# A new order of work and loads for the first two blocks of an attention, MoE and expert-mixture kernel

## The chip, the cores and the metric

The kernel runs on one core of one Trainium2 chip. The metric is the device time of one execution in microseconds, the median of three runs. A core has TensorE (PE, its weight loads shown as PEld), VectorE (DVE), ScalarE (ACT), GpSimd (POOL) and SyncE (SP, which here only issues transfers). Each engine carries out its own list of instructions strictly in the order in which the program wrote it, and waits on semaphores for what the others give it.

## The reference

All data are drawn at random; the attention part is linear, without a softmax.

```python
kv  = einsum('bhsd,bhse->bhde', k, v)          # q, k, v: (4, 8, 576, 64)
out = einsum('bhsd,bhde->bhse', q, kv)
out = out / sqrt(mean(out**2, -1) + 1e-6) * g_norm
x   = out as (2304, 512)
h   = max(x @ w1, x @ w2, x @ w3)              # (2304, 768), float64 weights
y   = h @ w_out                                # (2304, 512)
p   = probs / (probs.sum(-1) + 1e-9)
out = sum over 4 experts e of p[:, e] * (relu(y @ e_w1[e]) @ e_w2[e])
```

## The kernel before

The 2304 rows are worked on in six blocks of 384. The first stage does the attention of all rows, and beside it the first MoE for blocks 0 and 1; blocks 2 to 5 of the first MoE follow, then the expert mixture in 24 rounds. Only the first stage is touched by the change. It is a list of steps, one word each, in the string `steps`; a loop goes through it and writes the instructions of each step, so the string sets the order on every engine.

The steps of the attention, with the lines that issue them: **K**bc multiplies k and v of batch b for a pair of heads, c from 0 to 3, into PSUM bank 7 (L269, 20 products of 64x64 in the profile); after c = 3 four copies bring the bank into the tile `kvb` (L68, one 64x256 copy each). **T**g transposes tile g of q in two halves (L295, 8 products), each half copied out to `qT` (L68 on ACT, L70 on DVE). **O**g multiplies `qT` and `kvb` into two banks (L319, 16 products; L311 for the half tiles 2 and 7), squares the result on ACT (L332) and sums the squares on DVE (L333, L334). **N**g takes the root on ACT (L342) and scales the banks on DVE (L343 to L346, then L353 twice). **X**g transposes the scaled tile (L362, 8 products, 4 for a half tile) and copies it out with the gain `g2` as a factor (L366 on ACT, L368 on DVE) to `yT`. Letters behind a dot name the engines of a step's copies: a for ACT, v for DVE, p for POOL, and so K13.vvaa has its first two kvb copies on DVE.

`g2` is loaded from `g_norm` by two small transfers that follow the first call of `pump()`, and is doubled on DVE:

```python
pump()
for h in range(2):
    nc.sync.dma_start(out=g2[h * D : (h + 1) * D, :], in_=g_norm.rearrange("(d o) -> d o", o=1))   # L660
nc.vector.tensor_scalar(out=g2, in0=g2, scalar1=2.0, scalar2=None, op0=ALU.mult)                    # L661
```

The first MoE in this stage: **S**j splits block j of x into a high and a low part (L70, L376), **A**ijf makes the product of block j with slice f of weight i (L247, 12 products of 128x384; i = 0 is copied out, 1 and 2 are combined by a maximum on DVE, L392), **H**jf splits the maximum (L70, L401), and **P**f multiplies it with w_out (L413, 12 products). The weights come as float64, 24 pieces of 512 KB (L176 to the tiles `stage`). Each is converted by a scaling on ACT (L197) and a minimum on POOL (L198), then three integer operations on DVE (L205, L206, L209), then split into a high part (L68 or L70) and a low one (L183). In the kernel before, step a takes one piece through its split and the next through its first part, and step b does the DVE work.

All loads go through SP in the order of the string `order` (k, q or w for a weight piece): a load waits for its buffer, and eight transfers can be under way before SP waits for the oldest of them. `pump()`, called after each step, issues all loads whose buffers are free. After the loop PE goes on with block 2 (the row at 165.74 us below).

Of the kernel before, what the change touches and what calls it, by code (L numbers as in the profile page):

```python
# [8 lines left out]
F32 = mybir.dt.float32  # L9
# [12 lines left out]
def tile_attn_moe_moe2(  # L22
# [23 lines left out]
    nc = tc.nc  # L46
    B, H, S, D = q.shape
    NT, DM = out.shape
    FF = w1.shape[1]
    E, _, EF = e_w1.shape  # L50
    P = 128
# [3 lines left out]
    T = 384  # L55
# [3 lines left out]
    NPAIR = H // 2  # L59
    KC = S // P  # L60
    EPS = 1e-6

    def f32(ap):
        return ap.bitcast(F32)

    def copy(eng, out, in_):
        if eng == "a":
            nc.scalar.activation(out=out, in_=in_, func=AF.Copy)  # L68
        else:
            (nc.vector if eng == "v" else nc.gpsimd).tensor_copy(out=out, in_=in_)  # L70
# [7 lines left out]
    banks = [ps.tile([P, 512], F32, name=f"bank{n}") for n in range(8)]  # L78
# [7 lines left out]
    ident = cst.tile([P, P], F32, name="ident")  # L86
# [14 lines left out]
    def part(t, at, n, c=None):  # L101
        ap = t[:, at : at + n]
        return ap if c is None else ap.rearrange("p (c f) -> p c f", c=c)
# [13 lines left out]
    for b0 in range(0, B, 2):  # L117
        for b, s0 in ((b0, 0), (b0, 256), (b0, None), (b0 + 1, 0), (b0 + 1, 256)):
# [3 lines left out]
            else:  # L122
                rows = out[b * S + s0 : b * S + s0 + 256, :].rearrange("(p r) d -> r p d", r=2)
# [3 lines left out]
    kv_sb = {}  # L127
# [18 lines left out]
    HALF = P // 2  # L146
    KS = P * KC

    def load_kv(pool, b, c):
        for src, nm in ((k, "k"), (v, "v")):  # L150
            t = pool.tile([P, 4, KC + 1, D], F32, tag="kv", name=f"{nm}{b}_{c}", bufs=6)
            rows = src[b, 4 * c : 4 * c + 4]
            nc.sync.dma_start(out=t[:, :, 0:KC, :], in_=rows[:, 0:KS, :].rearrange("h (p c) d -> p h c d", c=KC))
            nc.sync.dma_start(out=t[0:HALF, :, KC, :], in_=rows[:, KS:S, :].rearrange("h p d -> p h d"))  # L154
            kv_sb[nm, b, c] = t
# [3 lines left out]
    worder = [("a", 0, 0)]  # L159
    for f in range(NF):  # L160
        worder += [("a", 1, f), ("a", 2, f)] + [("a", 0, f + 1)] * (f + 1 < NF) + [("o", 0, f)]
    N1 = 4 * NF
# [16 lines left out]
    def split_h(w, t, eng="a"):  # L179
        copy(eng, w[:, 0, :], t)  # L180

    def split_l(eng, w, t, key):
        eng.tensor_tensor(out=w[:, 1, :], in0=t, in1=f32(w[:, 0, :]), op=ALU.subtract)  # L183
        wt[key] = w

    def new_w(key):
        return w_buf[worder.index(key)]
# [4 lines left out]
    conv = {}  # L192

    def conv0(pool, key):
        words = stage[key].bitcast(I32).rearrange("p (n t) -> p n t", t=2)
        t = pool.tile([P, DM], F32, tag="cv", name="cv_" + "_".join(map(str, key)))
        nc.scalar.activation(out=t, in_=words[:, :, 1].bitcast(F32), func=AF.Abs, scale=2.0**-112)  # L197
        nc.gpsimd.tensor_scalar(out=t, in0=t, scalar1=EXP_TOP, scalar2=None, op0=ALU.min)  # L198
        conv[key] = t

    def conv1(pool, key):
        cpos[2] += 1
        words = stage.pop(key).bitcast(I32).rearrange("p (n t) -> p n t", t=2)
        ti = conv[key].bitcast(I32)
        nc.vector.tensor_scalar(out=ti, in0=ti, scalar1=3, scalar2=None, op0=ALU.logical_shift_left)  # L205
        nc.vector.scalar_tensor_tensor(  # L206
            out=ti, in0=words[:, :, 0], scalar=29, in1=ti, op0=ALU.logical_shift_right, op1=ALU.bitwise_or
        )
        nc.vector.scalar_tensor_tensor(  # L209
            out=ti, in0=words[:, :, 1], scalar=-(2**31), in1=ti, op0=ALU.bitwise_and, op1=ALU.bitwise_or  # L210
        )

    cpos = [0, 0, 0, 0]

    def conv_a(pool, eng="ap"):

        rest = []
        if cpos[3] < cpos[2]:  # L220
            key = worder[cpos[3]]
            w, t = new_w(key), conv.pop(key)
            split_h(w, t, eng[0])
            cpos[3] += 1
            if eng[1] == "p":
                split_l(nc.gpsimd, w, t, key)
            else:
                rest.append(lambda: split_l(nc.vector, w, t, key))
        if cpos[2] < cpos[1]:
            key1 = worder[cpos[2]]  # L230
            rest.insert(0, lambda: conv1(pool, key1))
        if cpos[1] < cpos[0]:
            conv0(pool, worder[cpos[1]])
            cpos[1] += 1
        return rest

    def load_w_to(pool, n):
        while cpos[0] < min(n, N1):
# [60 lines left out]
    def att_O(pool, kvb, gi):  # L299
# [30 lines left out]
        for i in range(nbank):  # L330
            sq = xt[:, i]
            nc.scalar.activation(out=sq, in_=o[i], func=AF.Square)  # L332
            nc.vector.reduce_sum(out=ss[:, i, :], in_=sq, axis=AX.X)  # L333
        nc.vector.tensor_scalar(out=a, in0=ss, scalar1=1.0 / D, scalar2=EPS, op0=ALU.mult, op1=ALU.add)  # L334
        xtok[gi] = (xt, ss, a, o, dst, small)
# [45 lines left out]
    nm = [0]  # L381

    def moe1_a(i, j, f, xs, eng="a"):

        ps = bank("a")
        col_mm(ps[:, :T], wt["a", i, f], xs)
        if i == 0:
            ms[j, f] = part(fa, NB * KT + nm[0] % 2 * T, T)
            nm[0] += 1
            copy(eng, ms[j, f], ps[:, :T])  # L390
        else:
            nc.vector.tensor_tensor(out=ms[j, f], in0=ps[:, :T], in1=ms[j, f], op=ALU.max)  # L392
# [225 lines left out]
    with tc.manual_schedule():  # L618
        cv_cm = tc.tile_pool(name="cvp", bufs=3, reuse_waits="tile")
        cvp = cv_cm.__enter__()  # L620
# [2 lines left out]
        att_cm = tc.tile_pool(name="att", bufs=2, side="right")  # L623
        att = att_cm.__enter__()
        make_identity(nc, ident)
        nc.gpsimd.memset(eps, EPS)

        nc.scalar.activation(out=g2, in_=ident[:, 0:1], func=AF.Sqrt)
        kvb = [att.tile([P, H * P + P], F32, name=f"kvb{i}", bufs=1) for i in range(2)]
        for t in kvb:  # L630
# [1 line left out]


        order = (
            "k00 q0 k01 q1 q2 k10 k11 q3 q4 q6 k20 q5 k21 k30 k31 w w w q8 q9 w"
        ).split()
        free = {"q": 6, "k": 3}

# [28 lines left out]
        def new_acc(n):  # L667
            return [bank("acc") for c in range(n)]
# [7 lines left out]


        steps = (
# [8 lines left out]
        ).split()  # L687
        for st in steps:
            st, *en = st.split(".")
            kind, at = st[0], [int(x) for x in st[1:]]  # L690
            if kind == "T":
                att_T(xq, *at, *en)
                free["q"] += 1
            elif kind == "K":
                att_kv(kvb, *at, *en)
                free["k"] += at[1] % 2
            elif kind == "O":
                att_O(xq, kvb, *at)
                if at[0] == len(groups) - 1:
                    att_cm.__exit__(None, None, None)  # L700
                    wp = ctx.enter_context(tc.tile_pool(name="wp", bufs=1, side="right", reuse_waits="tile"))
                    wr.append(wp.tile([P, 16 * 2 * DM], F32R, name="wr"))
                    w_buf.extend(part(wr[0], n * 2 * DM, 2 * DM, 2) for n in range(16))
            elif kind == "X":
                att_X(*at, *en)
                if at[0] == len(groups) - 1:
                    xq_cm.__exit__(None, None, None)
                    hs_cm = tc.tile_pool(name="hs", bufs=NF, side="right", reuse_waits="tile")
                    hs = hs_cm.__enter__()
            elif kind == "N":  # L710
                att_N(*at)
            elif kind == "A":
                i, j, f = at
                moe1_a(i, j, f, xs[j], *en)
            elif kind == "H":
                j, f = at
                hidden[j, f] = moe1_split(hs if j else None, j, f, *en)
            elif kind == "P":
                acc = acc or new_acc(KD)
                moe1_o(*at, hidden.pop((0, *at)), acc)  # L720
            elif kind == "S":
                xs.append(split_x(*at, *en))
            elif kind == "a":
                rest = conv_a(cvp, *en)
            elif kind == "b":
                for fn in rest:
                    fn()
            pump()
        assert cpos[3] == N1
        cv_cm.__exit__(None, None, None)  # L730
        moe1_store(0, acc)
        xs = xs[2]
        h = moe1_h(None, 2, 0, xs)
# [12 lines left out]
        for j in range(2, NB):  # L746
            acc = new_acc(KD)
            for f in range(NF):
                if j > 2 or f:
                    h = moe1_h(None, j, f, xs)  # L750
# [36 lines left out]
        for e in range(E):  # L787
            for pr in range(NPR):
                n = (e * NSB - 1) * NPR + pr
# [11 lines left out]
        for n, (e, sb, pr) in enumerate(rounds):  # L801
            last_sb = sb == NSB - 1
            more = not (e == E - 1 and last_sb)
            rest = iter(())
            if before is not None:
                e0, sb0, pr0 = before
                rest = second(n - 1, pr0)
# [60 lines left out]
```

## Time and profile before

| | |
|---|---|
| median of 3 runs | 1148.13 us (1147.34 to 1148.51) |
| the profiled execution: its own time | 1146.83 us |
| the profiled execution: span | 1145.0 us |
| PE busy in the span | 1120.5 us (98%), 6096 products |
| DVE / ACT / POOL busy | 562.7 / 390.9 / 236.8 us |
| the first stage, up to the first product of block 2 | 165.74 us |

The span runs from the first to the last instruction; the profiled execution's own time is 1.8 us longer. A busy share over the whole span says little about the first stage, which has other limits than the rest, so the rows below cut the span at the places where its limits change.

### The profile page before, as it was taken

What the parts mean: (1) busy time and instruction counts of PE and PEld (TensorE: products, weight loads), DVE (VectorE), ACT (ScalarE), POOL (GpSimd) and SP (SyncE); (2) the same over time, 40 slices, a digit from 0 to 9 for tenths busy, and PEclk for the clock granted to TensorE, in tenths of its full rate; (3) what the DMA queues carried; (4) which work ended last, traced back from release to release, by engine and by line L of the source; (5) the groups of instructions that cost most, each with busy time, mean ns of one, the idle gap of its engine ahead of it and who ended that gap; (6) DMA issues with size and microseconds to landing.
All of it is one profiled execution on the core that took longest, in us unless ns stands there. A gap on an engine that the chain in (4) does not pass through costs nothing.

```text
span 1145.0 us, 15032 instructions
## 1 busy us (share of the span) xinstructions
PE 1120.5 (98%) x6096; PEld 1031.7 (90%) x6096; DVE 562.7 (49%) x842; ACT 390.9 (34%) x699; POOL 236.8 (21%) x178
## 2 busy tenths in 40 slices
PE   6999899999999999999999999999999999999998
PEld 5888899999999888889888988888888888888887
DVE  1889862222325544344754436573535576343523
ACT  3653321121113434253634233452424253332321
POOL 1356740000401320205220202412020522011000
PEclk9999999999999999999999999999999999999999
DMA  9934410000201402014140403332030625040111
GB/s 255 283 107 130 147 47 29 1 28 1 65 29 37 157 1 102 9 56 138 60 171 1 165 1 131 127 122 99 29 138 9 212 65 193 1 153 14 48 63 56
DMA packets 77990, 99.59 MB, mean 87 GB/s; under 512 B 10336, under 2 KB 53344, under 8 KB 77920
## 3 DMA queue, kind: packets, MB, share of 16 engines
q1 hardware_dynamic: 77920, 98.62, 27.0%
q8 instruction: 48, 0.79, 0.3%
q14 instruction: 22, 0.18, 0.0%
HBM read 75.01 MB, written 23.59 MB: 86 GB/s over the span
## 4 chain that ended last, share of the span: by engine, by line
PE 88%; DVE 5%; DMA 2%; SPq 2%; ACT 1%; issue 1%; POOL 1%; DVEq 0%; ACTq 0%
PE bank L575 35%; PE bank L535 30%; PE bank L247 15%; PE bank L413 6%; DMA v<-in_v_dram 1%; DVE cv_a L206 1%; DVE cv_a L209 1%; PE bank L269 1%; DMA k<-in_k_dram 1%; PE bank L362 1%; DVE cv_a L205 1%; SPq L154 0%; PE bank L319 0%; DVE fa L392 0%; SPq L135 0%
## 5 line engine op out<-in xcount | busy, mean ns | idle before, releaser
L575 PE MATMUL bank<-wr,hr 128*128 128x512 f32 x792 | 227.0, 395 | 0.0
L559 DVE TENSOR_TENSOR fa<-bank,fa 128x384 f32<-128x384 f32 x144 | 80.1, 557 | 212.5 <-ACT fa L556 119.2
L575 PEld LDWEIGHTS bank<-wr,hr 128*128 128x128 f32 x792 | 147.0, 188 | 20.7
L517 POOL TENSOR_TENSOR fa<-fa 128x768 f32<-128x768 f32 x48 | 97.3, 2037 | 300.2 <-DMA fa<-y_d 243.0
L247 PE MATMUL bank<-xr,wr 128*128 128x384 f32 x792 | 145.2, 340 | 5.6 <-DVE fa L392 2.2
L247 PEld LDWEIGHTS bank<-xr,wr 128*128 128x128 f32 x792 | 139.6, 188 | 8.4 <-DVE fa L392 3.2
L486 POOL TENSOR_TENSOR w1s<-w1s 128x256 f32<-128x256 f32 x64 | 53.9, 862 | 421.8 <-DMA w1s<-in_moe_w_dram 374.7
L556 ACT ACTIVATE fa<-bank 128x384 f32<-128x384 f32 x144 | 70.6, 490 | 194.3 <-PE bank L535 194.3
L535 PE MATMUL bank<-rb,wr 128*128 128x384 f32 x648 | 131.5, 338 | 0.3 <-DVE hr L543 0.3
L535 PE MATMUL bank<-xr,wr 128*128 128x384 f32 x648 | 131.6, 338 | 0.0
L535 PEld LDWEIGHTS bank<-rb,wr 128*128 128x128 f32 x648 | 116.6, 188 | 10.2 <-DVE hr L543 0.6
L535 PEld LDWEIGHTS bank<-xr,wr 128*128 128x128 f32 x648 | 116.7, 188 | 9.6
L575 PE MATMUL bank<-wr,xr 128*128 128x512 f32 x324 | 100.8, 396 | 0.0
L392 DVE TENSOR_TENSOR fa<-bank,fa 128x384 f32<-128x384 f32 x72 | 39.8, 555 | 117.7 <-PE bank L247 117.5
L247 PE MATMUL bank<-xr,wl 128*128 128x384 f32 x504 | 90.5, 335 | 0.0
L247 PEld LDWEIGHTS bank<-xr,wl 128*128 128x128 f32 x504 | 87.4, 188 | 0.2 <-DVE wl L183 0.2
L575 PE MATMUL bank<-wl,hr 128*128 128x512 f32 x288 | 86.3, 394 | 0.0
L543 DVE SCALAR_TENSOR_TENSOR hr<-fa,hr 128x384 fp32r<-128x384 f32 x72 | 50.0, 695 | 42.6 <-ACT hr L542 42.6
L575 PEld LDWEIGHTS bank<-wr,xr 128*128 128x128 f32 x324 | 60.7, 188 | 10.8
L542 ACT ACTIVATE hr<-fa 128x384 fp32r<-128x384 f32 x72 | 37.8, 525 | 77.4 <-DVE fa L559 77.4
L575 PEld LDWEIGHTS bank<-wl,hr 128*128 128x128 f32 x288 | 53.4, 188 | 6.9
L542 ACT ACTIVATE xr<-fa 128x384 fp32r<-128x384 f32 x48 | 25.2, 525 | 96.7 <-DVE fa L559 96.7
(132 smaller groups left out, 1477.5 us busy)
## 6 DMA issues: line engine op xcount, KB each, us to landing
fa<-y_d SPq DMA_DIRECT2D x22, 768.0 KB, 6.2
stage_a<-in_moe_w_dram SPq DMA_DIRECT2D x18, 512.0 KB, 3.4
o_d<-fa SPq DMA_DIRECT2D x36, 256.0 KB, 3.7
fa<-o_d SPq DMA_DIRECT2D x36, 256.0 KB, 5.3
w1s<-in_moe_w_dram SPq DMA_DIRECT2D x32, 256.0 KB, 3.1
w2s<-in_moe_w_dram SPq DMA_DIRECT2D x32, 256.0 KB, 4.0
y_d<-fa SPq DMA_DIRECT2D x6, 768.0 KB, 3.8
o_d<-ob SPq DMA_DIRECT2D x18, 256.0 KB, 2.0
```

What stands on the lines that cost most here:

```text
L205: nc.vector.tensor_scalar(out=ti, in0=ti, scalar1=3, scalar2=None, op0=ALU.logical_shift_left)
L247: nc.tensor.matmul(ps, w[:, wi, c * P : (c + 1) * P], x[xi][:, c, :], start=(n == 0), stop=(n == 3 * KD - 1),)
L392: nc.vector.tensor_tensor(out=ms[j, f], in0=ps[:, :T], in1=ms[j, f], op=ALU.max)
L413: nc.tensor.matmul(acc[c][:, :T], w[:, wi, c * P : (c + 1) * P], h[hi], start=(f == 0 and n == 0), stop=(f == NF - 1 and n == 2),)
L486: eng.tensor_tensor(out=st[:, o], in0=st[:, a], in1=st[:, b], op=ALU.subtract)
L517: eng.tensor_tensor(out=yb[:, o], in0=yb[:, a], in1=yb[:, b], op=op)
L535: nc.tensor.matmul(out, w[wi][:, c * P : (c + 1) * P], y[yi][:, c, :], start=(i == 0 and k in BEGIN), stop=(i == 5), skip_group_check=k no ...
L542: nc.scalar.activation(out=h[0], in_=src, func=AF.Relu)
L543: nc.vector.scalar_tensor_tensor(out=h[1], in0=src, scalar=0.0, in1=f32(h[0]), op0=ALU.max, op1=ALU.subtract)
L556: nc.scalar.activation(out=s[k // 2], in_=a, func=AF.Copy)
L559: nc.vector.tensor_tensor(out=t, in0=x, in1=t, op=ALU.add)
L575: nc.tensor.matmul(banks[i], h[a, i // TPB][hi][:, i % TPB * P : (i % TPB + 1) * P], w[a][wi], start=(pr == 0 and a == 0 and m == 0), stop ...
```

## The change

Three things are new. Sixteen products of the identity matrix with itself are put ahead of everything on PE. The first k and v are loaded in parts by a function of their own, two of the parts issued by ACT's queue instead of SP's. And the two strings are written anew: the steps a and b are replaced by c (ACT and POOL part of a conversion), d (DVE part) and s (split), each with the number of its weight piece, and the engines of many copies are others.

```diff
+    WARM = 16
+    def load_first(pool):
+        ends = []
+        for src, nm, eng in ((k, "k", nc.sync), (v, "v", nc.scalar)):
+            t = pool.tile([P, 4, KC + 1, D], F32, tag="kv", name=f"{nm}0_0", bufs=6)
+            rows = src[0, 0:4]
+            parts = [
+                (t[:, 2 * i : 2 * i + 2, 0:KC, :], rows[2 * i : 2 * i + 2, 0:KS, :].rearrange("h (p c) d -> p h c d", c=KC))
+                for i in range(2)
+            ]
+            eng.dma_start(out=parts[0][0], in_=parts[0][1])
+            eng.dma_start(out=t[0:HALF, :, KC, :], in_=rows[:, KS:S, :].rearrange("h p d -> p h d"))
+            ends.append(parts[1])
+            kv_sb[nm, 0, 0] = t
+        for o, i in ends:
+            nc.sync.dma_start(out=o, in_=i)
     def load_kv(pool, b, c):
+        if (b, c) == (0, 0):
+            return load_first(pool)
...
-    def conv_a(pool, eng="ap"):
...
+    def conv2(key, eng="ap"):
+        w, t = new_w(key), conv.pop(key)
+        split_h(w, t, eng[0])
+        split_l(nc.gpsimd if eng[1] == "p" else nc.vector, w, t, key)
...
         make_identity(nc, ident)
+        for _ in range(WARM):
+            nc.tensor.matmul(banks[3][:, 0:P], ident, ident, start=True, stop=True)
...
-            "k00 q0 k01 q1 q2 k10 k11 q3 q4 q6 k20 q5 k21 k30 k31 w w w q8 q9 w"
+            "q1 q0 k00 k01 w q2 k10 k11 q3 w q4 k20 k21 q6 q5 k30 k31 w w q8 q9"
...
-            "K00 T0 K01 K02 K03 T1 O0 O1 K10 a N0 T2.av b K11 a N1 K12 K13 T3.av O2 b X0 N2 O3 T4 X1 "
+            "K00 K01 T1.av T0 K02 K03.avav c0 O1 O0 N1 K10 N0 T2 K11 d0 X1 K12 K13.vvaa T3.av X0.vv O3 T4.va "
...
-        assert cpos[3] == N1
+        assert cpos[2] == N1
```

On DVE, the first rows of its list; the names carry the program's numbers (bank7 is the bank of K, qT1 the transposed tile 1), and what a row waits for stands in brackets. Before:

```order
L661 TENSOR_SCALAR g2_75<-g2_75 128x1 [waits DMAHW3_49,DMAHW2_49,Activation_49]
L333 TENSOR_REDUCE ss0_253<-xt0_244 128x8 [waits Activation_49] x2
L334 TENSOR_SCALAR a0_254<-ss0_253 128x16 [waits DVE_49]
L333 TENSOR_REDUCE ss1_269<-xt1_260 128x8 [waits Activation_49] x2
L334 TENSOR_SCALAR a1_270<-ss1_269 128x16 [waits DVE_49]
```

On DVE, the same place after the change, where L667 is the former L661, L71 the former L70 and L337 the former L333:

```order
L667 TENSOR_SCALAR g2_75<-g2_75 128x1 [waits DMAHW6_49,DMAHW5_49,Activation_49]
L71 COPY qT1_210<-bank5_71 128x512 [waits PE_49]
L71 COPY kvb0_140<-bank7_73 64x4x64 [waits Activation_49] x2
L337 TENSOR_REDUCE ss1_274<-xt1_265 128x8 [waits Activation_49] x2
L338 TENSOR_SCALAR a1_275<-ss1_274 128x16 [waits DVE_49]
```

One copy of qT1 and two of kvb0 now stand on DVE behind the doubling of g2; before, ACT did all of these.

On SP, the end of the loads of batch 0 and what follows (v0_1 is v of the second half of the heads of batch 0; the short tail of a head has a load of its own). Before:

```order
L153 DMA v0_1_139<-in_v_dram 128x4x256
L154 DMA v0_1_139<-in_v_dram 64x4x64
L139 DMA q1_142<-in_q_dram 128x8x128
L135 DMA q2_144<-in_q_dram 32x8x128 x4
L153 DMA k1_0_149<-in_k_dram 128x4x256
L154 DMA k1_0_149<-in_k_dram 64x4x64
L153 DMA v1_0_152<-in_v_dram 128x4x256
L154 DMA v1_0_152<-in_v_dram 64x4x64
L660 DMA g2_75<-in_g_norm_dram 64x1 x2
```

On SP, after the change, where stage_a_0_0 is the first weight piece:

```order
L173 DMA v0_1_159<-in_v_dram 128x4x256
L174 DMA v0_1_159<-in_v_dram 64x4x64
L196 DMA stage_a_0_0_162<-in_moe_w1_dram 128x4x128
L136 DMA q2_164<-in_q_dram 32x8x128 x4
L173 DMA k1_0_169<-in_k_dram 128x4x256
L174 DMA k1_0_169<-in_k_dram 64x4x64
L173 DMA v1_0_172<-in_v_dram 128x4x256
L174 DMA v1_0_172<-in_v_dram 64x4x64
L666 DMA g2_75<-in_g_norm_dram 64x1 x2
```

The two loads of g2 keep their place behind k1_0 and v1_0; one weight piece has come in ahead of them, and q1 has gone to the front of the list.

On PE, the first rows before (ident is the identity matrix):

```order
L269 MATMUL bank7_73<-v0_0_131,k0_0_128 64x64 x10
L295 MATMUL bank4_70<-ident_74,q0_134 128x128 x4
L295 MATMUL bank5_71<-ident_74,q0_134 128x128 x4
L269 MATMUL bank7_73<-v0_0_131,k0_0_128 64x64 x10
L269 MATMUL bank7_73<-v0_1_139,k0_1_136 64x64 x20
L295 MATMUL bank6_72<-ident_74,q1_142 128x128 x4
L295 MATMUL bank4_70<-ident_74,q1_142 128x128 x4
L319 MATMUL bank0_66<-kvb0_124,qT0_168 128x128 x4
```

On PE, the same place after the change (a product of fp32 operands in K and O counts once here and twice in the profile):

```order
L631 MATMUL bank3_69<-ident_74 128x128 x16
L273 MATMUL bank7_73<-v0_0_151,k0_0_148 64x64 x20
L299 MATMUL bank4_70<-ident_74,q1_144 128x128 x4
L299 MATMUL bank5_71<-ident_74,q1_144 128x128 x4
L299 MATMUL bank6_72<-ident_74,q0_146 128x128 x4
L299 MATMUL bank4_70<-ident_74,q0_146 128x128 x4
L273 MATMUL bank7_73<-v0_1_159,k0_1_156 64x64 x20
L323 MATMUL bank0_66<-kvb0_140,qT1_210 128x128 x4
```

The sixteen identity products come first, both halves of k0_0 are multiplied at once, and O1 (L323) with kvb0 and qT1 is now ahead of O0.

## Rows read from the trace of the kernel before

**Rows 1.** Busy time by stage: stretch, its length, each engine, clock, DMA share, GB/s.

```profile
core 0: us, PE busy (x) PEld busy (x) DVE busy (x) ACT busy (x) POOL busy (x), PEclk, DMA share, GB/s
0.00:7.56 7.56, 0.00 (x0) 0.03 (x1) 0.00 (x0) 1.49 (x2) 2.71 (x9) 1.00 0.73 195
7.56:23.00 15.44, 14.53 (x129) 13.06 (x129) 0.00 (x0) 5.58 (x11) 1.04 (x1) 1.00 1.16 273
23.00:27.50 4.50, 3.04 (x56) 2.57 (x57) 3.55 (x11) 1.73 (x4) 0.00 (x0) 1.00 1.18 284
27.50:59.03 31.53, 28.26 (x356) 25.28 (x353) 25.38 (x53) 21.02 (x43) 11.35 (x5) 0.95 1.13 280
59.03:165.74 106.71, 101.24 (x596) 96.93 (x597) 95.47 (x151) 41.83 (x76) 70.68 (x51) 1.00 0.32 105
165.74:1145.00 979.26, 973.39 (x4969) 893.80 (x4968) 438.29 (x629) 319.25 (x564) 151.02 (x112) 1.00 0.22 74
```

**Rows 2.** Waits of PE in the first 200 us: total, times, longest.

```profile
PE bank L269 <- DMA v<-in_v_dram: 11.3, 4, 7.6
PE bank L247 <- DVE fa L392: 2.2, 3, 1.5
```

**Rows 3.** Timeline of PE: start, length, line, operation.

```profile
9.59 1.94 PE L295 MATMUL bank<-ident,q 128*128 128x128 f32 x8 [0.49 <-DMA q<-in_q_dram]
18.09 4.97 PE L319 MATMUL bank<-kvb,qT 128*128 128x128 f32 x32
23.00 0.95 PE L269 MATMUL bank<-v,k 128*64 128x64 f32 x20
...
51.29 1.09 PE L362 MATMUL bank<-ident,xt 128*128 128x128 f32 x8
52.22 1.95 PE L319 MATMUL bank<-kvb,qT 128*128 128x128 f32 x16
...
59.03 1.07 PE L295 MATMUL bank<-ident,q 128*128 128x128 f32 x8 [1.21 <-DMA q<-in_q_dram]
...
148.78 2.28 PE L247 MATMUL bank<-xr,wr 128*128 128x384 f32 x12
...
165.74 4.49 PE L247 MATMUL bank<-xr,wl 128*128 128x384 f32 x25
```

**Rows 4.** Timeline of DVE: its first instructions, and one step N.

```profile
23.78 0.15 DVE L661 TENSOR_SCALAR g<-g 128x1 f32<-128x1 f32 x1 [23.78 <-ACT xt L332]
23.85 1.27 DVE L333 TENSOR_REDUCE ss<-xt 128x8 f32<-128x512 f32 x2
...
59.78 0.25 DVE L343 RECIPROCAL rr<-s 128x16 f32<-128x16 f32 x1 [1.43 <-ACT s L342]
...
60.84 1.29 DVE L353 TENSOR_TENSOR xt<-bank,rr 128x512 f32<-128x512 f32 x2
```

**Rows 5.** Timeline of SP: the two loads of g_norm are issued.

```profile
16.57 1.19 SPq L660 DMA_DIRECT2D g<-in_g_norm_dram  x2
```

**Rows 6.** The loads of L660 alone.

```profile
DMA to landing us min/median/max: 6.2/6.4/6.5
```

**Rows 7.** The loads of L176, the weight pieces, alone.

```profile
DMA to landing us min/median/max: 3.3/3.4/8.8
```

**Rows 8.** Groups of DVE in the first 166 us: count, busy us, mean ns, idle.

```profile
L206 DVE SCALAR_TENSOR_TENSOR cv_a<-stage_a,cv_a 128x512 int32<-128x512 int32 x18 | 18.2, 1012 | 0.6
L209 DVE SCALAR_TENSOR_TENSOR cv_a<-stage_a,cv_a 128x512 int32<-128x512 int32 x18 | 15.1, 837 | 0.6
L392 DVE TENSOR_TENSOR fa<-bank,fa 128x384 f32<-128x384 f32 x24 | 13.0, 550 | 6.1 <-PE bank L247 6.1
L205 DVE TENSOR_SCALAR cv_a<-cv_a 128x512 int32<-128x512 int32 x18 | 12.1, 675 | 0.8 <-POOL cv_a L198 0.8
L70 DVE COPY qT<-bank 128x512 f32<-128x512 f32 x2 | 1.4, 682 | 0.0
```

**Rows 9.** Group of ACT in the first 166 us: the copies to kvb.

```profile
L68 ACT ACTIVATE kvb<-bank 64x256 f32<-64x256 f32 x16 | 6.1, 378 | 11.5 <-PE bank L269 11.3
```

More of the change, by code (lines that the diff above doesn't have):

```diff
@@ L211, in conv1 @@
         )
-    cpos = [0, 0, 0, 0]
-    def conv_a(pool, eng="ap"):
[L219 to L235, printed above, removed]
+    cpos = [0, 0, 0]
+    def conv2(key, eng="ap"):
+        w, t = new_w(key), conv.pop(key)
+        split_h(w, t, eng[0])
+        split_l(nc.gpsimd if eng[1] == "p" else nc.vector, w, t, key)
     def load_w_to(pool, n):
@@ L689, in tile_attn_moe_moe2 @@
             st, *en = st.split(".")
-            kind, at = st[0], [int(x) for x in st[1:]]
-            if kind == "T":
+            kind = st[0]
+            at = [int(st[1:])] if kind in "cds" else [int(x) for x in st[1:]]
+            if kind in "cds":
+                n = at[0]
+                if kind == "c":
+                    conv0(cvp, worder[n])
+                elif kind == "d":
+                    conv1(cvp, worder[n])
+                else:
+                    conv2(worder[n], *en)
+            elif kind == "T":
                 att_T(xq, *at, *en)
@@ L722, in tile_attn_moe_moe2 @@
                 xs.append(split_x(*at, *en))
[L723 to L727, printed above, removed]
             pump()
-        assert cpos[3] == N1
+        assert cpos[2] == N1
         cv_cm.__exit__(None, None, None)
```

15 rows, old and new, of the table steps are left out of this document.

## The prediction

> **What bounds the kernel now.** I read the busy time by stage first [rows 1]. Behind 165.74 us PE is busy for 973.39 of 979.26 us, and the change touches nothing there, so all it can win or lose lies in front of the first product of block 2 at 165.74 us [rows 3]. There PE loses time in two ways. Up to 59.03 us the transfers bound it: the DMA share is over 1 from 7.56 us on, the loads run at 273 to 284 GB/s, and 11.3 us of PE's waits are for v [rows 1, 2]. The last of these loads lets T8 begin at 59.03 us [rows 3]. From there to 165.74 us PE is busy for 101.24 of 106.71 us [rows 1]; the 5.5 us that are missing are mostly waits for a maximum on DVE or for a weight piece that DVE converted too late (2.2 us of them are for L392 [rows 2]); DVE is busy for 95.47 us of this stretch. So the new order can win what it takes from these 5.5 us, and whatever it loses before T8 moves the end as soon as the loads no longer hide it.
>
> **The part that decides: what stands at the head of DVE's list.** DVE's first instruction is the doubling of g2 (L661, afterwards L667), which waits for the two small loads of g_norm. SP issued these at 16.57 us [rows 5], each took 6.2 to 6.5 us to land [rows 6], although it carries a quarter of a KB, and DVE began at 23.78 us [rows 4]. The row puts that wait down to ACT; the order names the two loads, and 16.57 us, plus half of the 1.19 us for issuing the second, plus 6.2 to 6.5 us fits it. Before the change nothing on PE hung on it: ACT made all copies of qT and kvb for batch 0. Now the second half of qT1 and two of the four kvb copies stand on DVE behind it, and O1, the next product after K03 on PE, needs them. The two ACT copies of kvb are no way round, since the program lets the four wait for one another in turn.
>
> When do the loads of g2 land now? They keep their place on SP, with 512 KB (0.524 MB) of weights more in front of them. At 284 GB/s, the rate from 23.00 us on [rows 1], that is 1.85 us, so DVE starts at 23.78 + 1.85 = 25.6 us. Behind it come L667 (0.15 [rows 4]), the copy to qT1 (0.68 [rows 8]), a kvb copy on DVE, one on ACT (0.38 [rows 9]) and one on DVE. The trace has no kvb copy on DVE: 0.38 is one bound, as on ACT, 0.68 the other, as for DVE's copy of twice the columns [rows 8]; I take 0.4, near the first, as its columns are half of the second's. Together 2.0 us, and O1 starts at 27.6 us, where the kernel before had O0 at 18.09 us [rows 3]. PE has nothing to do from the end of K03 (about 17 us by my estimate; before, T1 follows it at once, and O0 at 18.09 us) to 27.6 us.
>
> The Trainium skill, DMA: Bandwidth & Descriptors, section Queues, rings and completion order, says that a transfer's semaphore is raised only after every earlier write of the same DMA engine, from all its queues. The 6.2 us for a quarter of a KB agree. The same page's section on the anatomy of one DMA fits a fixed cost of about 2.0 us, for transfers issued by GpSimd; by that alone, and as an estimate, g2 would land at 21.0 us and O1 start 4.6 us earlier than in my sum.
>
> **From O1 to T8.** Between O1 and T8 PE now has six O of 1.95 us (11.7), twelve K of 0.95 (11.4), five T and four X of 1.09 (9.8), the half X2 (0.55), the half O2 (about 1.1, between half an O and a whole X) and A000, which has moved ahead of T8 (2.28) [rows 3]: 36.8 us. T8 can start at 27.6 + 36.8 = 64.4 us if PE waits for nothing. The loads no longer hide this: the last one comes about 1.85 us later than before, at 59.03 + 1.85 = 60.9 us, since one more weight piece stands ahead of it.
>
> PE will wait, though, as DVE starts its list late too. First, O1 and O0 after ten idle microseconds: early in the trace the two O took 4.97 us, later one takes 1.95 [rows 3], though the clock column says 1.00, which is 2.4 GHz, in both places [rows 1]. I count 2 x 2.49 instead of 2 x 1.95, 1.1 us. Second, O3 needs kvb1, two of whose copies are on DVE behind N1, N0 and d0. O0 ends at 32.6 us, its last sum on DVE at about 33.8 us; N takes 2.35 us (59.78 to the end of L353 at 62.13 [rows 4]) and so N1 and N0 last until 38.5 us, d0 at 0.675 + 1.012 + 0.837 = 2.5 us [rows 8] until 41.0, two kvb copies until 41.8 and ACT's two until 42.6 us. PE reaches O3 at 27.6 + 1.1 and the 12.1 us of O1, O0, K10, T2, K11, X1, K12, K13, T3 and X0, at 40.8 us: 1.8 us. Third, the second banks of O4 and O5 wait for N3 and N4 in the same way, by my walk down both lists for 0.8 us in all. Together 3.7 us, T8 at 68.1 us. The bounds of this term are 0 and 7.2 us: if the slow rate lasts as long as at the start, the 14.53 us between 7.56 and 23.00 us [rows 1] against 9.9 us at the later rates (four K, two T, two O) say 4.6 us instead of 1.1.
>
> **From T8 to the end of the stage.** The work behind T8 is the 101.24 us of before [rows 1], less A000 (2.28), plus X5 (1.09), which now comes later: 100.05 us, to 168.15 us without a wait. The waits there were 5.5 us. Two weight pieces now come in among the first loads, so less conversion is left behind T8, and PE comes to T8 nine microseconds later and meets results that DVE has finished. POOL gets more of the splits, which could eat this up. Bounds 0 and 5.5 us; I take 0.5, near the lower end. The stage ends at 168.6 us, 2.9 us later than at 165.74.
>
> As a check from DVE alone: it is busy for 3.55 + 25.38 + 95.47 = 124.4 us from its start to 165.74 us [rows 1], the new list has as many rows but one, and at the same share of busy time a start 1.85 us later gives 1.85 us at the end. Both say slower by little.
>
> **The other parts.** The sixteen identity products cost 16 x 1.94 / 8 = 3.9 us at the early rate [rows 3]; they lie between 1.3 us and the first k, which came at 7.56 us, and cost nothing. What they may bring, faster products for K00 to K03, ends in the wait for g2. The same holds for the first k and v in parts and the ACT queue: the DMA engines are full at once [rows 1], and a K00 that starts one or two microseconds sooner or later (q1 and q0 now come ahead of it) is covered by the ten idle microseconds in front of O1. If that cover were not there, all of this would count in full.
>
> **The rivals.** *The load of g2 overtakes.* Faster. A small load may land as fast as a weight piece in a quiet queue, 3.3 us [rows 7]. Issued at 17.2 + 1.85 = 19.0 us it is there at 22.3, O1 starts at 24.3 and T8 at 61.1 us, just behind its load; with 1.1 us of slow products and 0.5 us later on, the stage ends at 162.75 us, 3.0 us earlier. It decides if g2 lands before some 23 us. Against it stand the 6.2 us of both loads [rows 6], for it that the quarters of q2 and the parts of k0_0 change how full the queues are. *The waits are hidden.* The same time. If O3 and O4 find what they need and DVE is never late behind T8, the stage ends at 64.4 + 100.05 = 164.45 us, 1.3 us earlier; with up to 3.6 us of waits in all it stays within what can be told. For it: the new order spreads the copies over three engines. Against it: DVE starts later than before and has as much to do. *The start drags on.* Much slower: the slow rate lasts (7.2 us) and DVE and POOL still make PE wait as before (5.5 us), 64.4 + 7.2 + 100.05 + 5.5 = 177.2 us, 11.5 us later.
>
> **How the numbers follow.** The sums are made against the profiled execution of 1146.83 us; the median of the runs is 1148.13 us, and I add the difference to that. Forecast: plus 2.9 us, 1151.0 us, chance 0.40. Overtaking: 1145.1 us, 0.15. Hidden waits: 1146.8 to 1150.4 us, 0.35. Dragging on: up to 1159.6 us, 0.10. A measurement of this kernel can tell about 0.2%, 2.3 us, from no change, so faster means under 1145.8 us and slower over 1150.4 us: 0.15, 0.35 and 0.50. The range from 1145.3 to 1156.0 us leaves out some of the first and of the last case; the forecast's own range, from 1150.0 to 1154.0 us, is that of its waits, one microsecond less or three more.
>
> **What would show it.** In the changed profile L667 should be DVE's first instruction at about 25.6 us, the first product of L323 should start at about 27.6 us after ten idle microseconds of PE that begin behind K03, T8 (L299, of q8) at about 68 us, and the first product of block 2 at about 168.6 us; the waits of PE for v should have shrunk, with a wait for a copy of kvb or qT as the longest in their place. I am wrong if L667 runs before 23 us, if O1 does not wait for it, or if PE stands at T8 by 62 us.

## The result, and the profile after

The changed kernel takes 1160.49 us (median of 4 runs, 1160.41 to 1160.63). Before, measured beside it, took 1147.74 us (4 runs, 1145.83 to 1148.51). The ratio is 1.0114, 95% interval 1.0096 to 1.0131: the change makes the kernel slower by 1.1%. The forecast was 1151.0 us with a range up to 1156.0 us, so its direction holds and its size does not.

The busy time by stage of the changed kernel, cut at its own turning points, in the columns of [rows 1]:

```profile
8.82:17.76 8.94, 6.16 (x57) 5.33 (x57) 0.00 (x0) 1.19 (x2) 0.00 (x0) 0.70 1.15 278
17.76:26.00 8.24, 2.40 (x41) 1.97 (x40) 1.17 (x3) 0.99 (x3) 0.00 (x0) 0.71 1.13 286
26.00:75.69 49.69, 39.78 (x440) 35.68 (x441) 40.74 (x77) 23.84 (x49) 19.62 (x13) 0.90 0.78 203
75.69:179.32 103.63, 99.23 (x593) 95.91 (x592) 98.11 (x136) 35.98 (x65) 81.15 (x60) 1.00 0.32 97
179.32:1158.60 979.28, 973.40 (x4969) 893.78 (x4968) 438.86 (x629) 319.45 (x564) 152.13 (x112) 1.00 0.22 74
```

The last row takes what it took before, 979.28 against 979.26 us. All that was lost lies in front of it: block 2 begins at 179.32 instead of 165.74 us, 13.58 us later. T8 begins at 75.69 us instead of 59.03 us, so the larger part was lost before T8. There the DMA share fell from 1.13 to 0.78: the loads no longer set the pace.

The waits of PE in the first 200 us of the changed kernel (total, times, longest), as in [rows 2]:

```profile
PE bank L323 <- DVE kvb L71: 5.8, 1, 5.8
PE bank L366 <- DVE xt L357: 4.3, 3, 2.7
PE bank L323 <- DVE qT L71: 4.2, 1, 4.2
PE bank L273 <- DMA v<-in_v_dram: 2.8, 1, 2.8
PE bank L366 <- ACT qT L69: 2.2, 1, 2.2
```

Before, 11.3 us were waits for v. Now 2.8 us are, and waits for copies and for DVE's scaling have taken their place. The timeline of PE shows where they lie (start, length, line, operation, number of products, idle time ahead), as in [rows 3]:

```profile
17.76 2.41 PE L273 MATMUL bank<-v,k 128*64 128x64 f32 x40
26.00 5.68 PE L323 MATMUL bank<-kvb,qT 128*128 128x128 f32 x32 [5.84 <-DVE kvb L71]
...
41.86 0.66 PE L366 MATMUL bank<-ident,xt 128*128 128x128 f32 x4 [2.23 <-ACT qT L69]
42.36 2.98 PE L323 MATMUL bank<-kvb,qT 128*128 128x128 f32 x16
...
58.04 0.63 PE L366 MATMUL bank<-ident,xt 128*128 128x128 f32 x4 [2.72 <-DVE xt L357]
...
66.42 1.64 PE L323 MATMUL bank<-kvb,qT 128*128 128x128 f32 x8 [4.20 <-DVE qT L71]
...
75.69 1.03 PE L299 MATMUL bank<-ident,q 128*128 128x128 f32 x8
...
179.32 6.40 PE L251 MATMUL bank<-xr,wl 128*128 128x384 f32 x36
```

K03 ends at 20.2 us, and PE stands 5.84 us before O1 at 26.00 us. The other three waits are that of X0 (2.23), X2 (2.72) and O5 (4.20). Now DVE's timeline, its head as in [rows 4] and two places further down:

```profile
24.75 0.15 DVE L667 TENSOR_SCALAR g<-g 128x1 f32<-128x1 f32 x1 [24.75 <-DMA g<-in_g_norm_dram]
24.82 0.68 DVE L71 COPY qT<-bank 128x512 f32<-128x512 f32 x1
25.53 0.42 DVE L71 COPY kvb<-bank 64x256 f32<-64x256 f32 x1
26.40 0.43 DVE L71 COPY kvb<-bank 64x256 f32<-64x256 f32 x1 [0.45 <-ACT kvb L69]
...
53.30 3.37 DVE L348 TENSOR_TENSOR rr<-a,rr 128x8 f32<-128x8 f32 x1
56.70 0.17 DVE L349 TENSOR_TENSOR rr<-rr,s 128x8 f32<-128x8 f32 x1
...
60.07 1.13 DVE L225 TENSOR_SCALAR cv_a<-cv_a 128x512 int32<-128x512 int32 x1
61.24 3.80 DVE L226 SCALAR_TENSOR_TENSOR cv_a<-stage_a,cv_a 128x512 int32<-128x512 int32 x1
65.08 0.69 DVE L229 SCALAR_TENSOR_TENSOR cv_a<-stage_a,cv_a 128x512 int32<-128x512 int32 x1
65.69 0.68 DVE L71 COPY qT<-bank 128x512 f32<-128x512 f32 x1
```

The two loads that this head waits for, in SP's timeline and, for their line alone, from issue to landing, as in [rows 5, 6]:

```profile
17.85 1.18 SPq L666 DMA_DIRECT2D g<-in_g_norm_dram  x2
```

```profile
DMA to landing us min/median/max: 6.2/6.4/6.5
```

They are issued 1.3 us later than before and take as long. The head is as forecast. The surprise is further down: in DVE's rows L348, a multiplication of eight columns, took 3.37 us, although the next row, of the same size, took 0.17. L226 took 3.80 us, L229 of the same shape 0.69. POOL's timeline shows what ran then:

```profile
53.21 3.43 POOL L380 TENSOR_TENSOR xr<-fa,xr 128x1536 fp32r<-128x1536 f32 x1
59.46 1.47 POOL L71 CAST xr<-fa 128x1536 fp32r<-128x1536 f32 x1 [2.82 <-ACT fa L370]
61.01 3.48 POOL L380 TENSOR_TENSOR xr<-fa,xr 128x1536 fp32r<-128x1536 f32 x1
```

Both long DVE instructions end within 0.6 us of the end of POOL's subtraction in S0 and S1, at 56.64 and 64.49 us. X2 waits for what stands behind the first, O5 for the copy to qT behind the second. The trace of before had the same pair, at a place where PE did not wait for DVE (DVE first, then POOL, kernel before):

```profile
39.73 2.27 DVE L334 TENSOR_SCALAR a<-ss 128x16 f32<-128x16 f32 x1
41.92 0.24 DVE L343 RECIPROCAL rr<-s 128x16 f32<-128x16 f32 x1
```

```profile
38.53 3.44 POOL L376 TENSOR_TENSOR xr<-fa,xr 128x1536 fp32r<-128x1536 f32 x1
```

The changed kernel has a third such place, just before its first stage ends, where S2 is split (one row each of DVE, POOL and PE):

```profile
174.05 2.76 DVE L71 CAST hr<-fa 128x384 fp32r<-128x384 f32 x1
```

```profile
173.12 3.48 POOL L380 TENSOR_TENSOR xr<-fa,xr 128x1536 fp32r<-128x1536 f32 x1
```

```profile
176.87 2.62 PE L417 MATMUL bank<-hr,wr 128*128 128x384 f32 x12 [1.22 <-DVE hr L71]
```

The next cast of this shape on DVE takes 0.36 us. The held one makes P5, the last step of the stage on PE, wait for 1.22 us. Before, DVE did the subtraction of S2 itself, in 1.75 us.

Two causes are therefore to be told apart: the head of DVE's list (the wait for g2), and POOL's subtraction holding DVE.

### The profile page after: what moved, and what is told of

The parts are those of the page before. It is cut to its first block, busy times and chain, and to the rows that moved or that the text cites. A ratio compares the mean times of both kernels' runs of the same rounds, so it can differ in the third digit from the quotient of the medians.

```text
span 1158.6 us, 15115 instructions
## 1 busy us (share of the span) xinstructions
PE 1126.8 (97%) x6128; PEld 1038.3 (90%) x6128; DVE 578.9 (50%) x843; ACT 383.0 (33%) x683; POOL 255.6 (22%) x193
## 4 chain that ended last, share of the span: by engine, by line
PE 88%; DVE 7%; DMA 2%; issue 2%; SPq 1%; ACT 1%; POOL 0%; DVEq 0%; ACTq 0%; POOLq 0%
PE bank L579 35%; PE bank L539 30%; PE bank L251 15%; PE bank L417 6%; DVE cv_a L226 1%; PE bank L323 1%; DVE cv_a L225 1%; DMA stage_a<-in_moe_w_dram 1%; DMA k<-in_k_dram 1%; DVE xt L357 1%; DMA g<-in_g_norm_dram 1%; DVE rr L348 1%; DVE fa L396 1%; PE bank L366 0%; DVE cv_a L229 0%
## 5 line engine op out<-in xcount | busy, mean ns | idle before, releaser
L417 PE MATMUL bank<-hr,wr 128*128 128x384 f32 x300 | 57.4, 339 | 1.2 <-DVE hr L71 1.2
```

The source lines that it names most:

```text
L417: nc.tensor.matmul(acc[c][:, :T], w[:, wi, c * P : (c + 1) * P], h[hi], start=(f == 0 and n == 0), stop=(f == NF - 1 and n == 2),)
```

## The experiments

The ratios are to runs of before on the same chip in the same comparison, with the 95% interval; "stage end" is the first product of block 2 in the profile.

**1. The loads of g_norm first, on ACT's queue.**

```diff
+        nc.scalar.dma_start(out=g2[...], in_=g_norm...)   # x2, ahead of the first pump()
         pump()
-            nc.sync.dma_start(out=g2[...], in_=g_norm...)
+    tbl = cst.tile([P, 1], F32, name="tbl")
-        nc.scalar.activation(out=g2, in_=ident[:, 0:1], func=AF.Sqrt)
+        nc.scalar.activation(out=tbl, in_=ident[:, 0:1], func=AF.Sqrt)
```

> The changed kernel with one thing moved: the two loads of g_norm are issued first, on ACT's queue (the square root that only loads ACT's table writes to a tile of its own, so that they need not wait for it). Theory: in the changed kernel O1 stands until 26.0 us because DVE's list begins with the doubling of g2, which waits for loads that land at 24.7 us. Then here DVE's doubling runs before 10 us, O1 starts about 1.7 us behind K03 (20.2 + 1.7 = 21.9 us), the sums and N1 come 4 us sooner, and the time falls by 3 to 5 us against the changed kernel, to 1155.5 to 1157.5 us. It stays over the kernel before, since the waits at X2 (2.7 us) and O5 (4.2 us), behind DVE instructions of 3.4 and 3.8 us, stay. Rival: these later waits set the end of the load stage by themselves, through the loads that wait for K21; then an earlier O1 is given back and the time stays at 1159 to 1161 us.

Measured: 1150.73 us, ratio 1.0018 (1.0009 to 1.0028), stage end 172.22 us. DVE's head and the first O on PE:

```profile
7.32 0.15 DVE L668 TENSOR_SCALAR g<-g 128x1 f32<-128x1 f32 x1 [7.32 <-DMA g<-in_g_norm_dram]
```

```profile
21.70 0.49 PE L324 MATMUL bank<-kvb,qT 128*128 128x128 f32 x2 [0.99 <-DVE kvb L71]
22.57 3.62 PE L324 MATMUL bank<-kvb,qT 128*128 128x128 f32 x30 [0.39 <-DVE kvb L71]
```

The same two loads land by 7.3 us when they are ahead of the others, and O1 starts 4.3 us earlier. The waits of X2 (2.1 us) and O5 (4.2 us) stay, as do long instructions on DVE (3.37 and 3.80 us). So the head of DVE's list is one cause, and not that of the other waits. The gain is greater than the 3 to 5 us expected: the stage end alone comes 7.1 us earlier, and O1 and O0 take 4.1 us after one microsecond of waiting, not 5.7. Another part, some 2 us behind the stage, is explained by experiment 9.

**2. The copies of batch 0 back on ACT**, so that O1 needs nothing from DVE.

```diff
-"K00 K01 T1.av T0 K02 K03.avav c0 ...
+"K00 K01 T1 T0 K02 K03 c0 ...
```

> The changed kernel with T1.av and K03.avav made T1 and K03, so that ACT makes all copies of qT1 and kvb0, as before the change; the loads of g_norm stay late. Theory that DVE's head of list is what O1 waits for: O1 starts at about 22 us, 4 us sooner, DVE still starts at 24.7 us but then has the squares ready and gets N1 done about 3 us sooner; 1156.5 to 1158.5 us. Rival that the kvb copies were late for another reason (the bank, or ACT's order): O1 stays at 26 us and the time at 1160.5 us.

Measured: 1154.23 us, ratio 1.0048 (1.0031 to 1.0065), stage end 173.51 us. O1 starts at 17.66 us, but X1 now stands for 2.81 us, as DVE still begins at 25.44 us. Part of the wait only moved; at the stage end 5.8 us of 13.6 are won, where 2 to 4 were expected.

**3. S0 and S1 on ACT and DVE instead of POOL.**

```diff
-... S0.pp ... S1.pp ...
+... S0.av ... S1.av ...
```

> The changed kernel with S0.pp and S1.pp made S0.av and S1.av: the high part of x is made by ACT, the low part by DVE, nothing of the two steps on POOL. Theory: the two POOL subtractions of 3.43 and 3.48 us (128x1536) hold up a DVE instruction each (a 128x8 product of 0.17 us took 3.37 us, L226 of 0.69 us took 3.80 us), and PE waits 2.7 us at X2 and 4.2 us at O5 for what stands behind these. Then both go, DVE gets 2 x 1.75 us of its own work for it, and the time falls by 3 to 6 us, to 1154.5 to 1157.5 us. Rival: the long DVE instructions waited for something else and DVE is just full; then 3.5 us more work on it make the time longer, 1162 to 1164 us.

Measured: 1155.81 us, ratio 1.0061 (1.0046 to 1.0076), stage end 174.45 us. DVE at the two places:

```profile
53.03 0.17 DVE L348 TENSOR_TENSOR rr<-a,rr 128x8 f32<-128x8 f32 x1
...
57.05 0.69 DVE L226 SCALAR_TENSOR_TENSOR cv_a<-stage_a,cv_a 128x512 int32<-128x512 int32 x1
...
58.82 1.76 DVE L380 TENSOR_TENSOR xr<-fa,xr 128x1536 fp32r<-128x1536 f32 x1 [0.35 <-ACT xr L69]
```

L348 and L226 are back at 0.17 and 0.69 us, the wait of X2 is gone and that of O5 is 0.9 us, though DVE now does the subtractions itself, in 1.76 us instead of POOL's 3.4. The wait before O1 is still there (7.3 us). The second cause stands beside the first.

**4. Both, 1 and 3.**

> Both: g_norm early on ACT's queue, and S0.av, S1.av. If the two causes are separate and add up, the time is 7 to 10 us under the changed kernel, 1150.5 to 1153.5 us, still over the kernel before by what its slower products after idle time cost. If one hides the other it is near the better of the two single ones, 1154.5 to 1157 us. If the new order is good once both are gone, it falls under the kernel before, under 1146 us.

Measured: 1147.6 us, ratio 0.9989 (0.9978 to 0.9999). The ratios of 1 and 3 lie 0.0096 and 0.0053 under the 1.0114 of the change, that of both 0.0125, or 11.0, 6.1 and 14.4 us of 1149: less than the sum of the two, 17.1, but more than the 7 to 10 us that were expected of two separate causes. In the profile, of an execution of 1149.46 us, T8 starts at 64.33 us and the stage ends at 170.32 us. The loss is gone; some 2 us of the gain belong to the new tile and not to the early load (experiment 9).

**5. POOL's subtraction in four pieces.** If the hold belongs to an instruction, four short ones hold DVE four times for a shorter time.

```diff
+            for c in range(KD):
+                nc.gpsimd.tensor_tensor(out=xs[1][:, c], in0=yT[j][:, c], in1=f32(xs[0])[:, c], op=ALU.subtract)
```

> The changed kernel with each subtraction of S0.pp and S1.pp on POOL written as four instructions of 128x384 instead of one of 128x1536; the engine and the work stay. Theory: a DVE instruction that meets the POOL subtraction stands until that one POOL instruction ends. Then the two long DVE instructions (3.37 and 3.80 us) shrink to under 1.5 us each, the waits at X2 and O5 fall from 2.7 and 4.2 us to under 1 and 2 us, and the time falls by 3 to 5 us to 1155.5 to 1157.5 us, as when the split was taken off POOL. Rival: DVE is slowed by POOL's traffic in all, in pieces as in one; or waits for a semaphore of S; then the waits and 1160.5 us stay.

Measured: 1156.12 us, ratio 1.0062 (1.0042 to 1.0082), stage end 174.71 us. DVE, then POOL, at the first place:

```profile
52.29 0.93 DVE L348 TENSOR_TENSOR rr<-a,rr 128x8 f32<-128x8 f32 x1
53.26 0.93 DVE L349 TENSOR_TENSOR rr<-rr,s 128x8 f32<-128x8 f32 x1
54.22 0.20 DVE L350 RECIPROCAL rr<-rr 128x8 f32<-128x8 f32 x1
```

```profile
52.20 3.88 POOL L384 TENSOR_TENSOR xr<-fa,xr 128x384 fp32r<-128x384 f32 x4
```

Two DVE instructions are held for 0.93 us each, about one piece of POOL (3.88 / 4 = 0.97), and the next is not held though POOL is still at work. So the hold lasts as long as one POOL instruction and strikes some kinds of instruction (L348, L349, L226, and L334 of before), not the reciprocal L350. The Trainium skill, SBUF — State Buffer, section Terms, says that DVE and GpSimd share one pair of ports which is locked for a whole instruction, the loser blocking fully. The 3.37 us beside POOL's 3.43, and 0.93 beside 0.97, agree.

The waits of X2 and O5 fall to 0.45 and 2.95 us; the second was expected under 2, but L226 and L229 are held for 1.37 us each. S2 is in pieces here too: P5 starts at 172.59 us without a wait, and the stretch behind T8 takes 101.81 us instead of 103.63.

**6. Before, with the two kvb copies of K03 on DVE**, one part of the change done alone.

```diff
-"K00 T0 K01 K02 K03 T1 O0 ...
+"K00 T0 K01 K02 K03.avav T1 O0 ...
```

> The kernel before with one word changed: K03 made K03.avav, so that two of the four kvb copies of batch 0 stand on DVE behind the doubling of g2; order, loads and all else as before. Theory: PE then stands at O0 from 18.1 us until 24.9 us (g2 at 23.8, and two copies with one of ACT between), 6.8 us; some 3.3 us of that are given back at the loads (1.8 us at K22, 1.2 us at T8), and the rest moves the end: 2 to 5 us slower than before, 1150 to 1153 us. Rival: the load stage hides it all, and the time is that of before within 1 us.

Measured: 1153.85 us, ratio 1.0043 (1.0029 to 1.0057), stage end 172.71 us. PE at its first O:

```profile
26.09 6.39 PE L319 MATMUL bank<-kvb,qT 128*128 128x128 f32 x32 [7.16 <-DVE kvb L70]
```

These two copies alone, 0.42 us each, make O0 wait for 7.16 us in the old order and cost about 0.4%, or 4.8 us. The mechanism of the forecast is shown from both sides.

**7. The change without the identity products and without the first loads in parts** (WARM = 0, and load_first not called).

> The changed kernel without the sixteen identity products and with the first k and v loaded as before, by SP alone and whole; the new order of work and of loads stays. Theory that these two parts end in the wait for g2: the time stays at 1160.5 us within 1.5 us. If the early products matter (a slower rate at the start that lasts past O1), it is 1162 to 1165 us; if the loads in parts do harm, as K01 stood for v until 12.3 us, it is 1157 to 1159 us.

Measured: 1161.05 us, ratio 1.0103 (1.0081 to 1.0125), against 1.0114 (1.0096 to 1.0131) with them. K00 starts at 11.01 us, 2.2 us later, and O1 at 27.76 us after a wait of 8.22 us. The waits of X2 and O5 are 2.7 and 4.2 us as in the changed kernel. In this profile, of the longest of four executions, O1 starts 1.8 us and block 2 1.9 us later than in the changed kernel, but the two ratios can't be told apart: these two parts of the change are worth nothing that can be measured.

**8. Two that gave little: products that fill the wait, and pieces in the old order.** The first puts 24 identity products behind K03, to see whether O1 and O0 are slow because PE had stood still.

```diff
+                if at == [0, 3]:
+                    for _ in range(24):
+                        nc.tensor.matmul(banks[3][:, 0:P], ident, ident, start=True, stop=True)
```

> The changed kernel with 24 more identity products right behind K03, in the idle time in front of O1 (5.8 us of them at the slow rate of 1.94 us for 8, 3.3 us at the fast one). Theory that O1 and O0 are slow because PE stood idle (5.68 us instead of 3.9, clock 0.50): they take 3.9 to 4.3 us here, O0 ends 1.4 to 1.8 us sooner, and the time falls by 1 to 2 us, to 1158.5 to 1159.5 us. Rival: DVE's chain (g2, copies, sums, N1) sets the pace behind O1, its squares come only little sooner, and the time stays at 1160.5 us within 0.6 us.

Measured: 1159.9 us, ratio 1.0085 (1.0069 to 1.0101), stage end 178.17 us. PE, and the busy time by stretch with the clock in the third column from the end:

```profile
19.54 5.62 PE L714 MATMUL bank<-ident 128*128 128x128 f32 x48
26.64 0.49 PE L323 MATMUL bank<-kvb,qT 128*128 128x128 f32 x2 [1.48 <-DVE kvb L71]
27.52 5.24 PE L323 MATMUL bank<-kvb,qT 128*128 128x128 f32 x30 [0.39 <-DVE kvb L71]
```

```profile
26.00:28.00 2.00, 0.97 (x6) 0.78 (x7) 0.99 (x3) 0.93 (x2) 0.36 (x1) 1.00 1.21 260
28.00:30.00 2.00, 2.00 (x13) 2.00 (x12) 0.67 (x1) 0.60 (x1) 2.00 (x2) 0.53 1.13 320
```

O1 and O0 are as slow as without the filler (5.24 us for 30 products). The granted clock of 0.53 is nearly that of the lower of the two levels, 1.2 GHz, from 28 us on, after PE had been filled up to 25.2 us and had stood for 1.5 us. Why the filler does not prevent that stays open.

The second, experiment 1 and the pieces of experiment 5 in the kernel before:

> The kernel before with g_norm early and the two POOL subtractions of S in four pieces each. In the kernel before with g early a DVE instruction of 0.17 us still took 2.27 and 2.14 us beside these. Theory that each such stand costs PE something only if DVE is waited for then: DVE gets about 2 us back before 55 us, the time falls by 0 to 1.5 us against g early alone, to 1145 to 1146.5 us beside 1149. Rival: the four short POOL instructions cost POOL's own chain (A000 needs S0 and S1) more than they give, 1147 to 1148 us.

Measured: 1147.03 us, ratio 0.9980 (0.9969 to 0.9992), stage end 167.24 us. Nothing is won against the first kernel of experiment 9 (0.9977). But the hold is not gone: where that kernel had one DVE instruction of 2.27 us at the first subtraction, here three that take 0.17 or 0.18 us alone take 0.79, 0.77 and 0.92 us, and at the second two take 0.99 and 0.77 us in place of one of 2.14. DVE is held nearly as long in all, so this run does not show what the hold costs where PE does not wait for DVE.

**9. Where the gain of an early g_norm comes from in the old order.** First, experiment 1's edit in the kernel before:

> The kernel before with the two loads of g_norm issued first, on ACT's queue, and nothing else. There DVE's first sum started at 23.85 us although its square was ready at 20.7 us. Theory: DVE begins about 3 us sooner, and as DVE is behind time up to 130 us, the end comes 0.5 to 3 us sooner, 1146 to 1148.5 us beside 1149 of the kernel before. Rival: DVE's early work is hidden by the loads, which PE waits for at 27.3, 42.9 and 59.0 us, and the time does not change.

Measured: 1146.32 us, ratio 0.9977 (0.9966 to 0.9988), a gain. But its stage ends at 167.05 us, no earlier than before; the shorter part is the stretch behind it, 977.55 against 979.26 us, and so it is in all kernels with that edit (977.2 to 977.6). They share a second thing, the new tile `tbl`. The next kernel has that alone, the loads of g_norm where they were:

> The kernel before with one edit: the square root on ACT that loads the table writes a tile of its own instead of g2; the loads of g_norm stay where they were. The kernels with g_norm early all had this edit too, and the stretch behind their first stage took 977.2 to 977.6 us instead of 979.3 us. Theory 1 (what shortened that stretch is the new tile, not the early load): it takes 977.2 to 977.6 us here as well, DVE still starts at about 23.8 us, the first stage ends at 165.7 us, and the time is some 1.8 us under that of before. Theory 2 (the early load did it): the stretch takes 979.3 us and the time is that of before within 0.1%.

Measured: 1146.3 us, ratio 0.9983 (0.9974 to 0.9992). Its stages, with a stage end at 166.64 us:

```profile
0.00:166.64 166.64, 146.17 (x1129) 136.30 (x1130) 125.53 (x214) 71.30 (x136) 85.93 (x66) 0.99 0.60 162
166.64:1144.20 977.56, 971.49 (x4969) 892.64 (x4968) 436.91 (x629) 319.48 (x564) 153.63 (x112) 1.00 0.22 74
```

DVE begins at 24.00 us as before, and the same 4969 products behind the stage are busy for 971.49 instead of 973.39 us [rows 1]. In the profiles of all fourteen kernels the eight without the tile have 973.39 to 973.42 us there, the six with it 971.44 to 971.50. So the new tile, with the square root that writes it, did it, not the load. In the old order an early g_norm gives nothing that can be measured (0.9977 against 0.9983, in intervals that overlap), as nothing on PE waits there for the head of DVE's list. Of the gains of experiments 1 and 4 some 2 us belong to the tile too. Why one more tile of four bytes in each partition makes products two parts in a thousand shorter isn't known.

**10. The best version of the new order**: experiment 4, and K13.vvaa changed to K13.aaaa, so that the copies of kvb1 don't stand on DVE.

> The changed kernel with g_norm early and S0.av, S1.av, and K13.vvaa made K13.aaaa: all four copies of kvb1 on ACT, so that they no longer stand behind N1, N0 and the first conversion on DVE. Theory: the wait of 2.2 us at X0 (for ACT's copy of qT3, which stands behind two kvb copies that wait for DVE's two) goes, O3 starts about 2 us sooner, and the time falls by 0.5 to 2 us against 1147.6, to 1145.5 to 1147 us. Rival: that wait is off the path (the loads of batch 2 come at 39 to 43 us), and the time stays at 1147.6 us within 0.5 us.

Measured: 1145.95 us, ratio 0.9973 (0.9963 to 0.9983), stage end 167.66 us. PE at X0 and at T8:

```profile
34.91 0.66 PE L367 MATMUL bank<-ident,xt 128*128 128x128 f32 x4 [0.77 <-ACT qT L69]
...
63.22 1.06 PE L300 MATMUL bank<-ident,q 128*128 128x128 f32 x8 [1.29 <-DMA q<-in_q_dram]
```

X0's wait has gone from 2.2 to 0.77 us, and T8 again waits for its load, as in [rows 3]. It beats both kernels, but not the kernel before with the new tile alone (0.9983, in intervals that overlap): freed of most of its waits, the new order is as fast as the old one. P5 still waits 1.37 us here, as S2 is still subtracted on POOL; no run took that away from this version.

## Why the prediction was wrong in size

**The head of DVE's list: right.** Its first instruction, the doubling of g2, was to run at 25.6 us and did at 24.75; O1 was to start at 27.6 and started at 26.00. The loads were issued 1.3 us later, where 1.85 was counted for the added weight piece, and took 6.2 to 6.5 us again [rows 6]. Experiments 1, 2 and 6 confirm the cause. The sum was 1.6 us too dear here. PE stood for 5.84 us before O1 and not for ten, as K03 ended at 20.2 us and not at about 17.

**From O1 to T8: the step that failed, "Together 3.7 us, T8 at 68.1 us", bounds 0 and 7.2.** The stretch took 49.69 us, 12.9 more than its 36.8 us of work. Of that PE was idle for 9.9 us and busy for 3.0 us longer than the work as summed. (That sum was a little long, as neighbouring rows overlap: in experiment 10 the same 440 products, at a granted clock of 1.00, are busy for 36.00 us. By that the slower products cost 3.8 us.)

- The wait for kvb1 was put at 1.8 us and is 2.2, seen at X0 just ahead of O3. Right.
- The slow products after an idle time were put at 1.1 us, for O1 and O0 alone. Those two cost 1.8 (5.68 against 2 x 1.95), and O3 behind X0's wait another 1.0 (2.98); products behind O5's wait were slow as well. The granted clock was 0.50, the lower level, from 24 to 28, 44 to 46 and 68 to 70 us, each time behind one of these waits.
- For O4 and O5 0.8 us of waiting for N3 and N4 was counted. What came were 2.7 us at X2 and 4.2 us at O5, 6.9 us, because POOL's subtraction held DVE. That term was missing. The steps N were costed at the 2.35 us that one takes when nothing holds it, and the conversion at its mean in the kernel before, though before already showed L334 at 2.27 us beside POOL, and though the mean of 1012 ns for L206 [rows 8] lies far above the 0.69 us that such an instruction takes alone. Experiments 3 and 5 show the cause.

From 3.7 to 12.9 us is 9.2; less the 1.6 us of the earlier start, T8 came 7.6 us later than forecast.

**Behind T8: put at the wrong end.** 0.5 us of waiting was counted, with bounds 0 and 5.5. The trace has 4.4 us (99.23 busy of 103.63), less work by 0.8 us, and so the stretch was 3.1 us too short in the sum. That DVE would catch up here was only an argument; DVE is busy for 98.11 us of it, and all the waits of PE are for DVE. Of these 1.2 us are the wait at P5 beside S2's subtraction, which experiment 5 took away. What made the others was not tested; but L226 and L229 do the same work as L206 and L209 and took 1186 and 1029 ns in the mean, against 1012 and 837 [rows 8]. 7.6 and 3.1 make the 10.7 us between 168.6 and 179.32 us. (The waits of before were read a little wrong too: of the 2.2 us for L392, 0.6 lie behind 165.74 us.)

**The check from DVE alone failed for the same reason**: it took DVE's busy time as fixed. Up to the stage's end it is 1.17 + 40.74 + 98.11 = 140.0 us, not the 124.4 of before.

**The other parts: right.** The identity products took 5.8 us, not 3.9, but ended before the first k was there at 8.82 us. They and the first loads in parts cost and gain nothing that can be measured (experiment 7).

**The rivals.** "The load of g2 overtakes" did not happen. "The waits are hidden" did not either. "The start drags on" had the right sign and, at 177.2 us, nearly the right stage end, but by another sum: it took 7.2 us of slow products and 5.5 us behind T8, where 2.8 us of slow products at O1 to O3, 6.9 us of held DVE and 4.4 us behind T8 were measured. Its size was reached through a mechanism that it did not have.

## What to carry to other kernels

When a step is moved to an engine that has stood idle at the start, look first at what the head of that engine's list waits for: two copies of 0.42 us each made PE wait for 7 us here because two loads of a quarter of a KB stood behind all others in the queue. Give an instruction on DVE the duration it has beside POOL, not the one it has alone, wherever a long subtraction on POOL may fall on it and a product waits for the result; then move the POOL work or cut it in pieces. And when a kernel gains without its waits having changed, run the edit's side effects alone, as with the tile of experiment 9.

## What the runs showed of the hardware that was not expected

- A subtraction of 128x1536 on POOL (3.43 us) held a DVE multiplication of 128x8, otherwise 0.17 us, for 3.37 us; pieces of 128x384 held two of them for 0.93 us each.
- The same load of a quarter of a KB lands 6.2 to 6.5 us after its issue behind a full queue, and by 7.3 us of the span when it is issued first (experiment 1).
- One more tile of 512 bytes, with no other instruction changed but the target of one square root, shortened 4969 products from 973.39 to 971.49 us.
- Twenty-four products up to 25.2 us did not keep the clock up: at 28 to 30 us 0.53 of it was granted, after a wait of 1.5 us.
